# Two more token tiles through the VectorE transpose, one weight unit fewer prepared early, and a new instruction order

## The chip, the cores and the metric

One core of one Trainium2 chip. The metric is the time of one execution on the device in microseconds (us), lower is better. Three executions of the kernel before took 564.96, 565.62 and 566.87 us; the median is 565.62 us.

## The reference

The input x has 2048 tokens of 512 features. It is normalised over the features; the result goes through a linear attention block without a causal mask (32 heads of 16), and, beside it, through a gated feed-forward block of 1792 hidden features. The output is x plus the product of the two.

```
xn  = layernorm(x)                              # 2048 x 512
q, k, v = split(xn @ wqkv), 32 heads of 16
pq, pk = phi(q), phi(k)                         # phi(t) = (t + 1 if t > 0 else exp(t)) + 1e-6
kv  = sum over tokens of pk^T v, per head       # 16 x 16 each
z   = sum over tokens of pk
o   = (pq @ kv) / (pq . z + 1e-6)
s   = o @ wo
g   = silu((gelu(xn @ w_gate) * (xn @ w_up)) @ w_down)   # 512 -> 1792 -> 512
out = x + s * g
```

## The kernel before

**Numbers and products.** All large products are made from float32 values that are split into a high part (a ScalarE cast) and a low part (a VectorE or GpSimd subtraction); each product is three matmul passes: high by high, high by low, low by high. Most products are also done by a seven-product scheme for two-by-two blocks (Strassen in Winograd's form), so that many tiles are sums and differences of blocks, made on GpSimd, VectorE and ScalarE. `PRODUCTS` names the seven; their sums are built in the PSUM banks X, Y and Z, with ScalarE copies that carry one bank over to another (`seed`, `saved`, `esaved`).

**First stage (0 to about 130 us).** The 16 tiles of 128 tokens are taken as eight pairs n = 0 to 7; pair n holds the tiles of `tokens[n]`, so pair 3 is tiles 3 and 7. For each tile: `load_x` brings x in; `ln` makes the statistics on VectorE and the normalised tile `xn` (VectorE for pairs 0 and 1, ScalarE after that); `transp` turns xn, so that features lie on partitions (`xt`); `split_x` and `forms` make the high and low parts of xt and of its block sums T (into `Xh`, `Xl`); `rest`, `first_products` and `plain` make k and q; `gacc` adds up the product of pk with xn over all tokens (banks `gps`), from which kv and z follow. Two ways to turn a tile exist:

- n < TX: four TensorE transposes into a PSUM tile `pt` and a ScalarE copy of it to `xt`.
- n >= TX: xn is stored to DRAM (`xn_d`), loaded back with its rows in another place (`xq`), and `squares`, one VectorE instruction that transposes 32 x 32 blocks, gives `xt`.

Pairs listed in `XA` are turned by TensorE but normalised on ScalarE.

**Weights of the feed-forward.** The gate and up matrices are used in 14 units q = 0 to 13 of 256 columns (even: gate, odd: up). A unit is made by `sums_w` (one load, four GpSimd sums) and four splits (ScalarE high, VectorE low). The units in `EARLY` are made by `prep_early` during the first stage, through small tiles `we`, and stored to `w_d` in eight pieces; `prep_w` later loads each with one DMA. The other units are made by `prep_w` where they are first used, in one of three buffers, and then stored whole to `w_d`. All 14 are loaded from there in the second half.

**Feed-forward (from about 124 us on).** `ffn(1, ...)` treats 1024 tokens with units 0 to 13, `ffn(0, ...)` the others with units 14 to 27, which are the same weights loaded again. `quad` makes one unit's products (banks FX, FY, FZ), the gelu and the gate-by-up tiles h; `prep_d` and `down_strassen` make the down product of each pair of units (banks dX, dY, dZ, sums `acc`). Beside it, `den` and `turn` prepare the attention's denominator and the turned pq for each tile, and `attn` and `out_tile` finish the output.

**Order.** `Plan.do` records each operation with a number in the order in which the code makes it. The list `ORDER` at the head of the file then gives the sequence of these numbers; each engine's instructions, TensorE's among them, and all DMA issues (every one on SP's queue) are emitted in it. So an engine's queue is the list cut down to its own operations, and an instruction that waits holds back what is behind it on its engine. The `due` times in the code play no part once ORDER is fixed.

Of the kernel before, what the change touches and what calls it, by code (L numbers as in the profile page):

```python
# [292 lines left out]
def kernel(  # L293
# [242 lines left out]
    TX = 4  # L536
# [4 lines left out]
    def load_next():  # L541
        if xq:
            load_x(xq.pop(0))

    xns = {}
    XA = [(2, 6), (3, 7)]

    def ln(*ts):
        n = len(ts)
# [378 lines left out]
    EARLY = range(11,14)  # L928
# [539 lines left out]
```

## Time and profile before

| what | value |
|---|---|
| median of three runs | 565.62 us (564.96 to 566.87) |
| the profiled execution: time | 565.26 us |
| the profiled execution: span of its instructions | 563.3 us |
| granted TensorE clock, mean | 0.999 of full speed |
| VectorE, ScalarE, GpSimd busy | 86%, 63%, 39% of the span |
| DMA traffic | 143.71 MB, 255 GB/s over the span |

The profile calls TensorE PE (its weight loads PEld), VectorE DVE, ScalarE ACT and GpSimd POOL; SP issues the DMAs. `L442 PE ... FX<-Xh,w` is an instruction of line 442 that writes the tile FX and reads Xh and w; lines 398, 404 and 442 are helpers, so that tiles say more than lines. A row of a group gives the number of instructions, their durations in ns (least, median, most, or the mean), and times in us from the start of the span. Matmuls are pipelined: each is recorded with 379 ns, and they start some 215 ns apart.

### The profile page before, as it was taken

Reading aid. Unit: us, or ns where it says so; the run is one execution under the profiler, and the core shown is the slowest. Engines: PE = TensorE matmul, PEld = TensorE weight load, DVE = VectorE, ACT = ScalarE, POOL = GpSimd, SP = SyncE. Lnnn points to the kernel's source line nnn. Section 1 sums busy time; section 2 is a strip of 40 time slices with the busy share of each in tenths; the row PEclk is TensorE's granted clock in tenths of the full one; section 3 lists DMA queues with packets and bytes.
Section 4 is the critical chain, followed back from the end, with each engine's and each line's share of the span. In section 5 each row is a group of like instructions: output and inputs, shape, how many; then the busy total and the mean of one; then the engine's idle time right before and its main releaser. Section 6 shows DMA issues by size and latency. Waiting matters only on the chain.

```text
span 563.3 us, 7910 instructions
## 1 busy us (share of the span) xinstructions
PE 556.6 (99%) x2616; PEld 486.8 (86%) x2616; DVE 485.6 (86%) x769; ACT 356.3 (63%) x650; POOL 221.7 (39%) x245
## 2 busy tenths in 40 slices
PE   8999999999999999999999999999999999999997
PEld 7888888888988888888888888888888888888886
DVE  6999898876889889999998876985899696899997
ACT  5998868768477876654456275888536354565541
POOL 4636173346684675503563532130122221235200
PEclk9999999999999999999999999999999999999999
DMA  7449899889959872589575998798966726167767
GB/s 271 143 112 300 265 318 296 269 242 331 345 178 376 285 311 76 204 317 343 187 291 188 372 398 295 285 302 307 298 222 221 268 79 240 52 211 254 269 235 252
DMA packets 82362, 143.71 MB, mean 255 GB/s; under 512 B 5393, under 2 KB 50449, under 8 KB 78354
## 3 DMA queue, kind: packets, MB, share of 16 engines
q1 hardware_dynamic: 82322, 143.22, 73.9%
q8 instruction: 20, 0.33, 0.2%
q14 instruction: 20, 0.16, 0.1%
HBM read 89.19 MB, written 54.00 MB: 254 GB/s over the span
## 4 chain that ended last, share of the span: by engine, by line
PE 94%; DVE 4%; ACT 1%; issue 1%; DVEq 0%; ACTq 0%
PE FX L442 25%; PE dX L442 12%; PE FZ L442 12%; PE gps L442 7%; PE dY L442 6%; PE FY L442 6%; PE sps L442 6%; PE X L442 6%; PE dZ L442 3%; PE Z L442 3%; PE k L442 2%; PE q L442 2%; PE Y L442 1%; PE warm L472 1%; DVE acc L404 1%; DVE acc L1128 1%
## 5 line engine op out<-in xcount | busy, mean ns | idle before, releaser
L442 PE MATMUL FX<-Xh,w 128*128 128x512 f32 x448 | 126.4, 379 | 0.8 <-ACT fu L398 0.5
L442 PEld LDWEIGHTS FX<-Xh,w 128*128 128x128 f32 x448 | 84.5, 189 | 13.5 <-ACT fu L398 0.9
L1174 POOL TENSOR_TENSOR h<-h,g 128x512 f32<-128x512 f32 x28 | 39.2, 1401 | 135.4 <-DVE h L404 85.2
L398 ACT COPY dY<-dX 128x512 f32<-128x512 f32 x56 | 32.1, 573 | 61.7 <-DVE acc L1128 40.4
L442 PE MATMUL FX<-Xl,w 128*128 128x512 f32 x224 | 66.1, 379 | 0.0
L442 PE MATMUL FZ<-Xh,w 128*128 128x512 f32 x224 | 65.0, 380 | 0.0
L398 ACT COPY fu<-FX 128x512 f32<-128x512 f32 x56 | 32.7, 585 | 26.4 <-PE FX L442 19.7
L442 PEld LDWEIGHTS FZ<-Xh,w 128*128 128x128 f32 x224 | 42.2, 189 | 6.3 <-issue 0.4
L442 PEld LDWEIGHTS FX<-Xl,w 128*128 128x128 f32 x224 | 42.3, 189 | 6.0
L404 POOL TENSOR_TENSOR tmp<-raw 128x256 f32<-128x256 f32 x28 | 25.4, 914 | 52.5 <-DVE we L404 28.1
L404 POOL TENSOR_TENSOR sums<-draw 128x256 f32<-128x256 f32 x28 | 25.1, 900 | 50.1 <-DMA draw<-in_B_w_down 27.6
L404 DVE TENSOR_TENSOR hfl<-sums,hfh 128x512 fp32r<-128x512 f32 x56 | 40.1, 723 | 3.0 <-ACT hfh L398 3.0
L442 PE MATMUL dX<-hfl,dh 128*128 128x512 f32 x112 | 42.0, 379 | 0.0
L442 PE MATMUL dX<-hfh,dh 128*128 128x512 f32 x112 | 41.9, 380 | 0.0
L1128 DVE TENSOR_TENSOR acc<-acc,dX 128x512 f32<-128x512 f32 x48 | 32.5, 682 | 10.5 <-PE dX L442 10.3
L442 PE MATMUL dX<-hfh,dl 128*128 128x512 f32 x112 | 41.3, 379 | 0.0
L1128 DVE TENSOR_TENSOR acc<-acc,dY 128x512 f32<-128x512 f32 x48 | 32.6, 679 | 9.1 <-PE dY L442 9.1
L398 ACT CAST hfh<-sums 128x512 fp32r<-128x512 f32 x56 | 33.9, 617 | 7.1 <-DVE sums L404 5.7
L442 PE MATMUL FZ<-Xl,w 128*128 128x512 f32 x112 | 33.3, 379 | 0.0
L404 DVE TENSOR_TENSOR hfl<-h,hfh 128x512 fp32r<-128x512 f32 x42 | 30.0, 716 | 3.8 <-ACT hfh L398 2.5
L442 PE MATMUL FY<-Xh,w 128*128 128x512 f32 x112 | 32.7, 379 | 0.0
L398 ACT CAST hfh<-h 128x512 fp32r<-128x512 f32 x42 | 25.6, 618 | 7.3 <-PE dY L442 5.3
(221 smaller groups left out, 1475.7 us busy)
## 6 DMA issues: line engine op xcount, KB each, us to landing
w<-w_d SPq DMA_DIRECT2D x17, 1792.0 KB, 8.8
w_d<-w SPq DMA_DIRECT2D x11, 1792.0 KB, 9.2
draw<-in_B_w_down SPq DMA_DIRECT2D x14, 512.0 KB, 4.5
w_d<-we SPq DMA_DIRECT2D x18, 256.0 KB, 3.5
x<-in_A_x SPq DMA_DIRECT2D x16, 256.0 KB, 3.4
q_d<-qp SPq DMA_DIRECT2D x16, 256.0 KB, 3.9
qz<-q_d SPq DMA_DIRECT2D x16, 256.0 KB, 3.0
q<-q_d SPq DMA_DIRECT2D x16, 256.0 KB, 3.8
```

The source lines that it names most:

```text
L398: do("ACT", act(n, src.psum), lambda o, i: nc.scalar.copy(o, i), dst, src, name=name)
L404: do(eng, c, lambda o, p, q: getattr(e, f"tensor_{op}")(o, p, q), dst, a, b, name=name)
L442: nc.tensor.matmul(o if r is None else o[:, r], a, turned(b), start=first, stop=made == self.passes[r], skip_group_check=self.on or r is n ...
L472: nc.tensor.matmul(o, w, w, start=True, stop=True)
L1128: do("DVE", dve(D), lambda o, i: nc.vector.tensor_add(o, o, i), o, ps, name="acc")
L1174: do("POOL", pool(NC), lambda o, i: nc.gpsimd.tensor_mul(o, o, i), h, g, name="h")
```

## The change

Four things differ: `TX` is 3, so that pair 3 (tiles 3 and 7) is turned by way of DRAM and VectorE; `XA` loses that pair, since its normalisation now goes by the branch for n >= TX (also on ScalarE); `EARLY` is units 12 and 13, and unit 11 is made by `prep_w`, stored to `w_d`, in the feed-forward; and `ORDER` is another list, of 3615 entries in place of 3621. The entry numbers shift with the operations that come and go, and nearly every line of the list differs. Its first and last lines stand here for all:

```diff
 ORDER = [
-    3, 8, 0, 1, 4, 5, 6, 11, 10, 12, 56, 9, 7, 57, 58, 17, 15, 59, 16, 18, 60, 14, 19, 90, 20, 89, 22, 13, 92, 23, 94, 116, 21, 28, 100, 29, 118, 62,
...
+    3, 8, 0, 4, 959, 5, 6, 10, 11, 12, 56, 7, 9, 57, 1, 58, 17, 16, 59, 14, 18, 19, 60, 15, 20, 90, 89, 22, 21, 13, 94, 23, 28, 62, 61, 95, 63, 65,
...
+    3590, 3601, 3599, 3605, 3606, 3591, 3600, 3603, 3612, 3592, 3602, 3613, 3609, 3614, 3610, 3611,
 ]
...
     CL = 2
-    TX = 4
+    TX = 3
...
     xns = {}
-    XA = [(2, 6), (3, 7)]
+    XA = [(2, 6)]
...
-    EARLY = range(11,14)
+    EARLY = range(12,14)
     WHEN = (90, 140)
```

No function is new.

283 rows, old and new, of the table ORDER are left out of this document.

## The prediction

> **What bounds the kernel now.** I read the page first: span, busy times, the chain's shares. Then the waits of TensorE, the chain in order of time, and busy time by stretches.
>
> ```profile
> span 563.3 us, 7910 instructions
> PE 556.6 (99%) x2616; PEld 486.8 (86%) x2616; DVE 485.6 (86%) x769; ACT 356.3 (63%) x650; POOL 221.7 (39%) x245
> PE 94%; DVE 4%; ACT 1%; issue 1%; DVEq 0%; ACTq 0%
> ```
>
> TensorE is busy in 556.6 of 563.3 us, and 94% of the chain is its own. So a change is worth what it takes out of TensorE's instructions, plus what it alters in TensorE's few waits. Those are:
>
> ```profile
> PE warm L472 <- DVE neg_half L464: 1.1, 1, 1.1
> PE k L442 <- ACT b L398: 0.8, 1, 0.8
> PE FX L442 <- ACT fu L398: 0.5, 1, 0.5
> PE FX L442 <- ACT FY L398: 0.2, 1, 0.2
> ```
>
> The reader sees 1.5 us that a new order could win (0.8 in the front, 0.5 + 0.2 in the first feed-forward half); the 1.1 us ahead of the warm-up and the drain behind the last matmul stay. The chain, in order of time, shows where the 0.5 came from and what eight transposes cost:
>
> ```profile
> 12.39 0.87 PE pt L655 x8
> ...
> 285.42 1.69 DVE sums L404
> 287.14 0.62 ACT hfh L398
> 287.81 0.59 ACT fu L398
> 288.45 2.43 PE FX L442 x10
> ```
>
> A VectorE subtraction took 1.69 us, a ScalarE cast stood behind it, the copy that empties bank X behind that, and TensorE waited. VectorE is the second bound. In the rows below the columns are stretch, length, then busy time of PE, PEld, DVE, ACT, POOL:
>
> ```profile
> 15.00:30.00 15.00, 15.00 (x73) 13.13 (x73) 14.94 (x30) 14.56 (x28) 9.24 (x15) 1.00 0.50 144
> 30.00:45.00 15.00, 15.00 (x77) 13.17 (x76) 14.37 (x27) 14.22 (x24) 5.55 (x8) 1.00 0.43 115
> 180.00:200.00 20.00, 20.00 (x95) 17.50 (x94) 16.81 (x25) 16.80 (x34) 12.59 (x13) 1.00 0.79 274
> 200.00:220.00 20.00, 20.00 (x94) 17.53 (x93) 19.14 (x26) 13.97 (x28) 11.23 (x11) 1.00 0.66 253
> 220.00:240.00 20.00, 20.00 (x94) 17.50 (x93) 19.19 (x32) 12.27 (x23) 13.62 (x14) 1.00 0.40 145
> 240.00:260.00 20.00, 20.00 (x95) 17.50 (x94) 19.20 (x32) 10.90 (x20) 2.94 (x2) 1.00 0.92 330
> 260.00:280.00 20.00, 19.75 (x92) 16.80 (x91) 18.84 (x30) 8.99 (x17) 9.30 (x9) 1.00 0.70 232
> 280.00:300.00 20.00, 19.46 (x91) 16.73 (x90) 17.86 (x28) 10.80 (x21) 10.91 (x9) 1.00 0.79 293
> ```
>
> VectorE is nearly full in two places, 15 to 45 and 200 to 280, and the waits of 0.2 and 0.5 us lie at the end of the second.
>
> **How I read the new order.** Numbering the operations as the code makes them names every entry of both lists. Adding the trace's own durations along one engine's entries gives a count of work, no run: the *TensorE place* of an entry is the TensorE time listed ahead of it.
>
> **Part 1: pair 3 (tiles 3 and 7) by squares.**
>
> ```profile
> L655 PE MATMUL pt<-blk,xn x32: 272/273/273, 6.8 to 44.5; 128*128 128x128 f32 x32
> L398 ACT COPY xt<-pt x8: 573/590/621, 11.7 to 45.2; 128x512 f32<-128x512 f32 x8
> L629 DVE STREAM_TRANSPOSE xt<-xq x8: 1053/1095/1116, 49.6 to 102.7; 128x512 f32<-128x512 f32 x8
> ...
> x<-in_A_x SPq DMA_DIRECT2D x16, 256.0 KB, 3.4
> ...
> xn_d<-xn SPq DMA_DIRECT2D x8, 256.0 KB, 3.9
> xq<-xn_d SPq DMA_DIRECT2D x8, 256.0 KB, 3.2
> ```
>
> Four transposes per tile, 32 for eight tiles; two tiles fewer are eight, 0.87 us by the chain's row, all on TensorE's path: **-0.87**. ScalarE loses two copies (2 x 0.590 = 1.18), VectorE gains two squares (2 x 1.095 = 2.19), SP gains two stores and two loads. The new list puts the second store at TensorE place 32.7 and the squares at 41.4 and 42.7. Between lie 3.9 + 3.2 = 7.1 us of landing and two issues of some 0.4, so the round trip is covered by about 1 us; DMA share is 0.43 there. If that cover goes, the first square stands at VectorE's head with all of VectorE's queue behind it, and products of pair 2 wait: up to 1 us. On GpSimd the clearing of a column of tile 3's xn (place 35.9) now waits for that tile's store (31.8, landed some 4 us later); the next on GpSimd is pair 3's own T form, at 42.7. On SP the four issues stand among loads of x; the load that is held up longest, by the wait for the store, is at place 37.5, its tile's statistics at 49.4, and 3.4 us of landing fit. GpSimd's T forms follow the squares as they followed the copies. VectorE's 2.19 lies in its full stretch, which I price with the front.
>
> **Part 2: weights of unit 11 made in the feed-forward.**
>
> ```profile
> L404 POOL TENSOR_TENSOR tmp<-raw 128x256 f32<-128x256 f32 x28 | 25.4, 914 | 52.5 <-DVE we L404 28.1
> ...
> L404 DVE TENSOR_TENSOR w<-tmp,w x22: 677/688/1756, 123.6 to 249.7; 128x512 fp32r<-128x512 f32 x22
> L404 DVE TENSOR_TENSOR w<-raw,w x22: 412/679/1168, 117.9 to 246.5; 128x512 fp32r<-128x512 f32 x11, 128x256 fp32r<-128x256 f32 x11
> ...
> w<-w_d SPq DMA_DIRECT2D x17, 1792.0 KB, 8.8
> w_d<-w SPq DMA_DIRECT2D x11, 1792.0 KB, 9.2
> ```
>
> The same work moves from TensorE places 45 to 69 to places 230 to 280: four GpSimd sums (4 x 0.914 = 3.7), four ScalarE casts, four VectorE subtractions (2 x 0.688 + 0.679 + 0.412 = 2.47). SP loses eight small stores and one load of 1.8 MB and gains one store of it (9.2 us to land, at place 286; the next user of that buffer, unit 14's load, is at 310). What leaves the first stage wins nothing there, since TensorE does not wait between 10 and 265 us. What arrives could cost up to 2.47: in 200 to 260 the three rows leave VectorE 2.5 us free, in all three so thinly that little can be moved into them. But the new list takes other VectorE work out: two `den` reductions go from places 224 and 223 to 181 and 191, where the row leaves 3.2 free, and four `turn` pairs from 245 to 267 to 237 to 253. Counted along the lists, VectorE holds 58.7 of 60 us in 200 to 260 (58.1 before), 18.2 in 260 to 280 (18.7) and 19.9 in 280 to 300 (18.1). The tightest place: from the last matmul of a `dX` sum (first row half of the down product of units 2 and 3, place 221) to unit 9's first product (place 231), VectorE's queue holds 10.2 us, from the addition of that sum to the `h` whose release the product needs, where TensorE has 9.7. So a wait of about 0.5, one like it of 0.2 near 205, and some 0.3 of hand-over for each: 1.3 us. Against that, some durations counted there are stretched ones (rival C shows one); at the medians the queues would be shorter than TensorE's work and the wait nil. I take 1.2 us of waits where before had 0.7: **+0.5**. Ends: -0.7 (all gone) and +3.0 (rival C).
>
> **Part 3: the front, new order.** A slice, with idle time in brackets:
>
> ```profile
> 7.17 1.03 DVE L585 TENSOR_SCALAR xn<-x,mv,rstd 128x512 f32<-128x512 f32 x1
> 7.40 0.37 ACT L398 CAST Xh<-pt 128x256 fp32r<-128x256 f32 x1 [0.88 <-PE pt L655]
> 7.67 0.38 ACT L398 CAST b<-pt 128x256 fp32r<-128x256 f32 x1
> 8.19 0.45 PE L442 MATMUL k<-kq,b 128*128 128x512 f32 x1 [0.83 <-ACT b L398]
> 8.48 0.60 PE L655 MATMUL pt<-blk,xn 128*128 128x128 f32 x4
> 9.54 1.12 PE L442 MATMUL k<-kq,Xh 128*128 128x512 f32 x3
> ```
>
> TensorE waits 0.83 for the cast to b, behind another cast; the second tile's transposes come after. The new list puts b's cast first, that tile's normalisation ahead of another tile's statistics, and both tiles' transposes before any product, so the gap can fill with work. At most 0.83 is won. But counted to the first q products, VectorE's queue then leaves TensorE only 0.2 to 0.3 us (1.3 to 1.5 before), and it holds the 2.19 of squares soon after: I take half, **-0.4**; ends -0.83 and +0.5.
>
> **The rest.** From 310 us on no TensorE wait over 0.03 us shows, and the last two half sums are only swapped: 0, ends -0.1 and +0.5.
>
> **Sum.** -0.87 - 0.4 + 0.5 = -0.8: span 563.3 to 562.5. The profiled run took 565.26, 1.96 around its span; the median of the three is 565.62, 0.36 above it. From the median: **564.8 us**.
>
> **Rivals.** *B, all of it works:* -0.87 - 0.83 - 0.7 = -2.4, 563.2. For it: each of the waits has one named cause that the order can move. Against: the counts above.
> *C, slower: VectorE becomes TensorE's bound in 200 to 300.* For it:
>
> ```profile
> 285.17 1.38 POOL L965 TENSOR_TENSOR qz<-qz,zq 128x512 f32<-128x512 f32 x1
> 285.34 1.76 DVE L404 TENSOR_TENSOR sums<-h,sums 128x512 f32<-128x512 f32 x1
> ...
> L404 DVE TENSOR_TENSOR sums<-h,sums x28: 675/685/1760, 169.4 to 530.2; 128x512 f32<-128x512 f32 x28
> ```
>
> The subtraction that started inside GpSimd's multiplication took 1.76 instead of 0.685. Unit 11's four sums now run beside a full VectorE; if each stretches a VectorE instruction by its length, that is up to 3.7 us, less about 0.7 that the stretched ones there now give back: +3.0 for +0.5, so 567.3, and to 568.3 with the front's +0.5. It decides once waits there exceed about 3.7 us in all. Against: most instructions beside GpSimd keep 0.685, the median.
> [...]
> *D, the transposes' 0.87 buys nothing,* because VectorE, full at 15 to 45, sets the first stage and takes the 2.19 more: -0.4 + 0.5, so 565.7. [...] Against D: eight tiles go this way already, and no wait of TensorE follows them.
>
> **Chances.** "Same" is within 0.3%, 1.7 us, about what a measurement of this kernel can tell. The forecast, with D's 0.15, 0.49; B, or enough of it to pass -1.7, 0.28; C 0.23. So faster 0.28, same 0.49, slower 0.23. Range 563.0 to 567.9: from B nearly to C's end.
>
> **What would show it.** 24 transposes in PE's pt row and ten squares; PE busy near 555.7; TensorE's wait for b gone or halved; TensorE's waits in 200 to 330 listed behind DVE's `h`, `acc` or `sums`, 1 to 1.5 us in sum; den reductions before 195. Wrong if a DMA (xq, w or draw) appears among TensorE's releasers, if VectorE stretched by GpSimd costs over 3 us, or if waits appear after 330.

## The result, and the profile after

Six executions of the kernel after took 562.45 to 565.12 us, median 563.33; six of the kernel before 564.96 to 567.46, median 566.52. The ratio is 0.9949, 95% interval 0.9927 to 0.9971: faster by 2.9 us. That is beyond the 1.7 us that I had called "same". The time lies in the range, 0.3 us above its lower end: it is the time of rival B (563.2), not that of the forecast (564.8).

The profiled execution happens to be the slowest of the six, 565.12 us with a span of 563.1. Its page, first lines and chain shares:

```profile
span 563.1 us, 7880 instructions
...
PE 555.3 (99%) x2608; PEld 485.2 (86%) x2608; DVE 496.0 (88%) x771; ACT 354.2 (63%) x648; POOL 222.5 (40%) x245
...
PE 91%; DVE 4%; DMA 2%; issue 1%; SPq 0%; POOL 0%; DVEq 0%; POOLq 0%
```

TensorE has eight instructions less and is busy 1.3 us less (555.3; near 555.7 was expected). VectorE is busy 10.4 us longer (485.6 before), of which the two squares explain 2.2. TensorE's waits in this execution:

```profile
PE pt L655 <- DVE xn L585: 1.3, 1, 1.3
PE warm L472 <- DVE blk L462: 1.1, 1, 1.1
PE dX L442 <- DVE fifth L1128: 1.1, 1, 1.1
```

The waits for b, and for ScalarE's copies in 265 to 290, are gone. Two others have come, 1.3 us at 8 us and 1.1 us at 520 us, neither in a place that I had named. A second profile of the same kernel (the first experiment) has neither. Groups by tile and busy time by stretches (PE, PEld, DVE, ACT, POOL), kernel after:

```profile
L655 PE MATMUL pt<-blk,xn x24: 272/273/328, 6.2 to 27.9; 128*128 128x128 f32 x24
...
L629 DVE STREAM_TRANSPOSE xt<-xq x10: 1087/1098/1120, 42.3 to 98.1; 128x512 f32<-128x512 f32 x10
...
L404 DVE TENSOR_TENSOR sums<-h,sums x28: 662/684/1754, 167.8 to 527.9; 128x512 f32<-128x512 f32 x28
```

```profile
15.00:30.00 15.00, 15.00 (x75) 12.97 (x74) 14.64 (x30) 14.83 (x29) 9.91 (x17) 1.00 0.59 172
30.00:45.00 15.00, 15.00 (x70) 12.76 (x69) 14.97 (x26) 13.17 (x22) 6.10 (x9) 1.00 0.61 178
...
200.00:220.00 20.00, 20.00 (x94) 17.55 (x93) 18.54 (x28) 13.33 (x26) 13.58 (x14) 1.00 0.59 220
220.00:240.00 20.00, 20.00 (x94) 17.45 (x94) 19.55 (x33) 12.93 (x25) 12.28 (x14) 1.00 0.56 226
240.00:260.00 20.00, 20.00 (x95) 17.53 (x94) 19.84 (x31) 10.68 (x21) 6.71 (x6) 1.00 0.49 131
```

VectorE is nearly as full as counted, 57.9 of 60 us in 200 to 260 (58.7 was counted) and 19.84 of 20 in its last third, and yet TensorE has no idle time in any of these stretches: VectorE, busy for 97% of 200 to 260, cost TensorE no wait there. In the place that the prediction found tightest VectorE was even ahead: it waited 0.23 us for TensorE there (and 0.23 at 226.78 in after_again).

```profile
227.80 0.69 DVE L1128 TENSOR_TENSOR acc<-acc,dX 128x512 f32<-128x512 f32 x1 [0.23 <-PE dX L442]
```

To compare executions I use one count. Of TensorE's 2552 matmuls that are neither warm-up nor transposes I take the starts of number 20, 1000 and 1600, counted from 0 (they lie near 14, 222 and 352 us) and the end of the last, each less 0.109 us for every transpose ahead of it (0.87 us for the eight in the chain's row of before). The differences are TensorE's time for an equal number of matmuls, waits included, in us. Each row is one execution, the one that was profiled:

| execution | to the 20th | 20th to 1000th | 1000th to 1600th | to the end |
|---|---|---|---|---|
| before | 13.09 | 208.19 | 131.21 | 203.40 |
| after, profiled first | 12.62 | 209.12 | 129.81 | 204.74 |
| after_again | 12.27 | 208.45 | 130.20 | 203.14 |
| squares_back | 12.52 | 208.51 | 129.95 | 203.14 |
| old_front | 12.92 | 209.02 | 130.12 | 203.14 |
| front_on_dve | 12.03 | 208.48 | 129.72 | 203.14 |
| before_new_front | 11.92 | 208.80 | 130.35 | 203.13 |
| late_new | 13.05 | 211.01 | 129.70 | 203.14 |
| no_unit11 | 11.85 | 208.77 | 132.70 | 203.14 |
| no_unit11b | 12.51 | 208.52 | 130.84 | 203.13 |
| late_new_loaded | 13.12 | 208.74 | 135.84 | 203.13 |

### The profile page after: what moved, and what is told of

Read it like the earlier page. It is cut to its first block, busy times and chain, and to the rows that moved or that the text cites. A ratio compares the mean times of both kernels' runs of the same rounds, so it can differ in the third digit from the quotient of the medians.

```text
span 563.1 us, 7880 instructions
## 1 busy us (share of the span) xinstructions
PE 555.3 (99%) x2608; PEld 485.2 (86%) x2608; DVE 496.0 (88%) x771; ACT 354.2 (63%) x648; POOL 222.5 (40%) x245
## 4 chain that ended last, share of the span: by engine, by line
PE 91%; DVE 4%; DMA 2%; issue 1%; SPq 0%; POOL 0%; DVEq 0%; POOLq 0%
PE FX L442 26%; PE FZ L442 13%; PE dX L442 12%; PE gps L442 7%; PE FY L442 6%; PE dY L442 6%; PE X L442 6%; PE sps L442 3%; PE dZ L442 3%; PE Z L442 3%; PE k L442 2%; PE q L442 2%; PE Y L442 1%; DMA out_yT<-g 1%; DVE acc L1128 1%
## 5 line engine op out<-in xcount | busy, mean ns | idle before, releaser
L404 POOL TENSOR_TENSOR sums<-draw 128x256 f32<-128x256 f32 x28 | 23.2, 837 | 69.1 <-DMA draw<-in_B_w_down 46.1
L404 DVE TENSOR_TENSOR hfl<-sums,hfh 128x512 fp32r<-128x512 f32 x56 | 46.6, 837 | 0.7 <-ACT hfh L398 0.5
L404 DVE TENSOR_TENSOR hfl<-h,hfh 128x512 fp32r<-128x512 f32 x42 | 32.0, 763 | 0.2
```

What stands on the lines that cost most here:

```text
L404: do(eng, c, lambda o, p, q: getattr(e, f"tensor_{op}")(o, p, q), dst, a, b, name=name)
```

## Experiments

Three theories are tested. Theory 1 is the prediction's sum with its better ends: the transposes, the front and the waits in 200 to 300 us each give back what they cost. Theory 2 says that the waits at 8 and 520 us are meetings of VectorE and GpSimd that other executions don't have. Theory 3 says that the new order stands only with the move of unit 11. D is the prediction's rival. "Place" is TensorE time listed ahead of an entry, as there. Each ratio is to the kernel before on the same chip, with its 95% interval. The runs were made on three chips, on which the kernel before had medians of 565.40, 565.39 and 565.54 us, so medians are compared across them too.

**after_again.** The kernel after once more, without an edit.

> The kernel after, unchanged, for a second profile beside the three below. Theory 1 (the sum of the prediction with better ends: transposes -0.87, the waits of 0.24 + 0.54 us in 265 to 290 gone, and the rest a matter of the front): ratio 0.995 to the kernel before, the wait of about 1.3 us in the front there again. Theory 2 (the waits of 1.3 us in the front and 1.1 us at 520 us in the profiled execution are chance meetings of VectorE and GpSimd, which other executions don't have): same ratio, but at least one of the two waits is gone or under half, and the span is 560.4 to 562 us.

562.77 us, 0.9953 (0.9940 to 0.9965). Span 560.5. Besides the wait of 1.1 us ahead of the warm-up, TensorE has one wait:

```profile
PE dX L442 <- DVE hfl L404: 0.3, 1, 0.3
```

The front, first in the kernel after's first profile, then here (timeline: start, length; the GpSimd row of the first joins two instructions):

```profile
5.37 0.62 ACT L398 CAST kq<-wk 128x512 fp32r<-128x512 f32 x1 [3.31 <-DMA wk<-in_A_wqkv]
...
6.58 2.67 POOL L404 TENSOR_TENSOR kq<-wk,kq 128x512 fp32r<-128x512 f32 x2
...
6.64 1.48 DVE L585 TENSOR_SCALAR xn<-x,mv,rstd 128x512 f32<-128x512 f32 x1 [0.46 <-POOL rstd L558]
...
8.18 0.66 PE L655 MATMUL pt<-blk,xn 128*128 128x128 f32 x4 [1.28 <-DVE xn L585]
```

```profile
6.28 0.62 ACT L398 CAST kq<-wk 128x512 fp32r<-128x512 f32 x1 [4.22 <-DMA wk<-in_A_wqkv]
...
6.51 0.55 DVE L585 TENSOR_SCALAR xn<-x,mv,rstd 128x512 f32<-128x512 f32 x1 [0.46 <-POOL rstd L558]
...
6.98 1.27 POOL L404 TENSOR_TENSOR kq<-wk,kq 128x512 fp32r<-128x512 f32 x1 [0.50 <-DMA wk<-in_A_wqkv]
```

In the slower one the weights landed 0.9 us earlier. So GpSimd's subtraction started 0.06 us ahead of the second xn instead of 0.47 behind it; xn took 1.48 us, and the second transposes waited 1.28. In the eight profiles that have this front, xn took 1.48 in five, where the subtraction came first (ScalarE's cast at 5.03 to 5.37 us), and 0.55 in three (cast at 5.91 to 6.28). The first k product began at 8.81 to 9.04 or at 7.86 to 8.37. The wait at 520 us is in one profile of all: `sums` and `g` there took 1.75 and 1.76 us beside GpSimd's `dl`. Theory 2 holds for both: the first comes and goes with the landing of the weights, the second came once.

**squares_back.** Pair 3 by TensorE again, its entries at the old places:

```diff
-    TX = 3
+    TX = 4
...
-    XA = [(2, 6)]
+    XA = [(2, 6), (3, 7)]
```

> The kernel after with pair 3 turned by TensorE again (32 transposes, eight squares), its instructions at the places that the kernel before gave them; all else stays. Theory 1 (the transposes bound TensorE): 0.87 us slower than the kernel after, 564.2 where that has 563.3. Rival D (VectorE sets 15 to 45 us, so it gains what two squares of 1.1 us cost): within 0.3 us of the kernel after, and less idle time of TensorE between 10 and 60 us.

563.76 us, 0.9974 (0.9964 to 0.9984): 1.0 us over after_again by the medians, 1.2 +- 0.9 by the ratios. Its profile has the front's meeting too:

```profile
PE warm L472 <- DVE blk L462: 1.1, 1, 1.1
PE pt L655 <- DVE xn L585: 0.9, 1, 0.9
```

In the table its 20th to 1000th matmul takes 208.51, against 208.45 in after_again: in this pair of executions the two squares cost TensorE nothing, and the transposes' 0.87 is won in full. Rival D, for which squares_back was to lie within 0.3 us of the kernel after, falls, though by the ratios only just.

**weights_back and order_alone.** Unit 11 goes into the first stage again, under TensorE's new order, with the instructions of units 11 to 13 placed anew; order_alone also has squares_back's edit.

```diff
-    EARLY = range(12,14)
+    EARLY = range(11,14)
```

> The kernel after with unit 11's weights made in the first stage again and loaded in the feed-forward; TensorE's order stays, and the instructions of units 11 to 13 are put into the first stage where the queues have most room. Theory 1 (the move gives and costs nothing by itself): within 0.3 us of the kernel after. Theory 3 (the new order of the first stage has no room for a third unit, so the move is what lets it stand): TensorE waits in 40 to 140 us, 1 to 3 us in all, so 564.5 to 566.

> The new order alone: TensorE's order of the kernel after, with 32 transposes and eight squares, and with unit 11's weights made in the first stage as before. Theory 1: 0.87 us over the kernel after, 564.2, so two thirds of the gain. Theory 3 (the order needs the move): 565.5 to 567, with TensorE waiting in 40 to 140 us. If the order gives nothing and the two other parts carry the gain: 566.5, the time before, with the waits of 0.24 and 0.54 us in 265 to 290 us there again.

588.29 us, 1.0402 (1.0381 to 1.0423), and 597.33 us, 1.0570 (1.0544 to 1.0596): far beyond every theory. ScalarE's waits in 38 to 135 us, and busy time by stretches around one wait of TensorE, of weights_back:

```profile
ACT we L399 <- DMA w_d<-we: 15.4, 5, 4.8
```

```profile
83.00:86.20 3.20, 0.19 (x2) 0.10 (x1) 2.01 (x5) 1.30 (x3) 0.00 (x0) 1.00 0.14 52
86.20:88.00 1.80, 1.80 (x6) 1.04 (x7) 1.80 (x5) 1.80 (x4) 1.58 (x3) 0.77 0.88 282
88.00:90.00 2.00, 2.00 (x6) 1.53 (x6) 2.00 (x4) 1.96 (x5) 2.00 (x4) 0.50 0.83 270
```

ScalarE stood 15.4 us before casts into `we`, each behind the store that empties the tile, with all its other work queued behind. TensorE waited 3.0 us, and then ran at half its clock (0.50 in the row of 88 to 90). These two show that three units, as I packed them, don't fit into the new first stage; they don't price the order. How the 23 and 32 us come together wasn't followed further.

**order_alone2.** This is order_alone with the entries of units 11 to 13 spread wider.

> The new order alone once more: 32 transposes, unit 11's weights in the first stage as before, TensorE's order of the kernel after; this time the instructions of units 11 to 13 are spread with a landing of 4 us allowed for every store, since in the two kernels before ScalarE's casts waited up to 4.8 us for the store that empties their buffer. Theory 1 (order and transposes carry the gain, the move none): 563.7, 0.9 over the kernel after. Theory 3 (the new order has no room for a third unit in the first stage): waits of TensorE in 40 to 160 us of 1 us and more, 565 or above.

592.28 us, 1.0461 (1.0440 to 1.0481). ScalarE again waited 15.1 us for those stores. Whether some other placement of a third unit fits the new order stays open.

**old_front.** ORDER only: the old list up to place 12 us, then the new one.

```diff
 ORDER = [
-    3, 8, 0, 4, 959, 5, 6, 10, 11, ...    (new order, to place 12 us)
+    (the same operations in the old order)
     ... the new order
```

> The kernel after with the front of the kernel before: every instruction up to TensorE place 12 us in the old order, all behind it in the new one. Theory 1 (the new front wins 0.4 to 0.8 us): 0.4 to 0.8 us slower than the kernel after, so 563.2 to 563.6 where that has 562.8, with the wait for b of about 0.8 us there again. Rival (what the new front wins is given back whenever GpSimd stretches the second xn): within 0.2 us of the kernel after.

563.89 us, 0.9978 (0.9967 to 0.9989): 1.1 us over after_again by the medians (1.4 +- 0.9 by the ratios). TensorE's wait in the front is 1.1 us here, and not for b, as was expected:

```profile
PE k L442 <- POOL kq L404: 1.1, 1, 1.1
```

The table has 0.65 us of the difference before the 20th matmul and 0.57 behind it. The second figure is no more than the kernel after's two executions differ by there (209.12 and 208.45), so it need not be the front's.

**front_on_dve.** One subtraction of the front moved from GpSimd to VectorE, where it stands behind the second xn:

```diff
-        kq_split(0, wk1, k, eng="DVE" if k else "POOL")
+        kq_split(0, wk1, k)
```

> The kernel after with one subtraction of the front (the low part of kq, first half) on VectorE, behind both xn, not on GpSimd. Theory 2 (GpSimd's subtraction, when its operand lands early, starts before the second xn and stretches it from 0.55 to 1.48 us, and TensorE's second transposes wait 0.9 to 1.3 us): no such wait in the profile, under 0.3 us in all before 10 us; the time 0.2 to 0.5 us below the kernel after if the meeting comes in about half the executions, the same if it is rare. Rival (VectorE's 0.68 us more delays b by as much): a wait behind b, 0.3 us or more slower.

562.03 us, 0.9940 (0.9928 to 0.9952), span 559.8. The only wait of TensorE that the profile lists, then rows of the front:

```profile
PE warm L472 <- DVE blk L462: 1.1, 1, 1.1
```

```profile
6.61 0.55 DVE L585 TENSOR_SCALAR xn<-x,mv,rstd 128x512 f32<-128x512 f32 x1 [0.46 <-POOL rstd L558]
7.07 0.69 DVE L404 TENSOR_TENSOR kq<-wk,kq 128x512 fp32r<-128x512 f32 x1
```

The subtraction takes 0.69 us here, where GpSimd took 1.27, and fills a hole in which VectorE waited for ScalarE. The weights landed late in this execution (ScalarE's cast at 6.39 us), so the meeting would not have come anyway; that it can't come follows from the subtraction's place behind xn. This version beats the kernel before, and it has the lowest median of all; against the kernel after, 0.7 us by the medians, the intervals still overlap. Whether it beats that too stays open.

**no_unit11.** Unit 11 isn't made, and unit 12's stored weights are loaded in its place, so this kernel leaves out a part of the work:

```diff
-        if q in EARLY:
+        if q in EARLY or q == 11:
...
-            dma(w.map(lambda ap: ap.bitcast(F32)), w_d(q), 2220)
+            dma(w.map(lambda ap: ap.bitcast(F32)), w_d(max(q, 12)), 2220)
```

> The kernel after without the making of unit 11's weights: unit 12's stored weights are loaded in their place in both row halves, so unit 11's share of the output is another; four GpSimd sums, four ScalarE casts, four VectorE subtractions and one store are left out. Theory 1 (what arrives in the feed-forward is hidden behind TensorE): within 0.2 us of the kernel after. The prediction's price for it (+0.5, VectorE nearly full in 200 to 280): 0.3 to 0.5 us faster than the kernel after, with the wait of about 0.3 us near 273 gone.

567.22 us, 1.0020 (1.0004 to 1.0036): with less work, 4.4 us slower than after_again. VectorE's and TensorE's waits, then SP's issues, of no_unit11:

```profile
DVE q L1235 <- DMA q<-q_d: 2.6, 1, 2.6
...
PE dX L442 <- DVE acc L1128: 2.1, 1, 2.1
```

```profile
240.35 0.44 SPq L394 DMA_DIRECT2D w<-w_d  x1
240.84 0.44 SPq L394 DMA_DIRECT2D q<-q_d  x1
```

The q of 256 KB was issued 0.5 us behind a load of 1.8 MB. VectorE could use it at 249.59 us, 8.7 us later; in after_again, without that load, a q issued at 240.66 was there before 247.32, when VectorE came to it. VectorE stood, and with it the addition to `acc` that empties bank dX. The profiled execution is the fastest of twelve (564.64 us); what the others, up to 568.26, lost on top isn't seen. Seven of them, 566.96 to 568.26, have a mean granted clock of 0.997, the five faster ones 0.998 to 1.000; one fall of the clock, as the last section shows it, would make such a difference by my estimate (3.41 us at 0.50 are 0.003 of the span), so it is a likely part of the loss, though none of these seven was profiled.

**no_unit11b.** This is no_unit11 with the load one DMA issue later, behind that q.

> no_unit11 once more (unit 12's stored weights loaded in place of unit 11's, which are not made), with one change: the 1.8 MB load stands behind the small load of q, not ahead of it. If the place of the load made no_unit11 4 us slower than the kernel after (VectorE waited 2.6 us for a q issued 0.5 us behind the load, TensorE 2.1 us behind VectorE): 562.5 to 563, at most 0.3 us from the kernel after, and no wait of TensorE over 0.5 us near 250. If it is anything else that the load brings: 565 or above again.

563.62 us, 0.9969 (0.9956 to 0.9982): 3.6 us less than no_unit11, from the place of one DMA issue alone. TensorE's wait there is now

```profile
PE FZ L442 <- DVE h L404: 0.5, 1, 0.5
```

since the next store behind the load, `t_d` from `sums`, still held VectorE 1.3 us. So making unit 11 in the feed-forward costs nothing that shows: without it, and with the load at this better place, the kernel is no faster than after_again (0.9 +- 1.0 us slower).

**late_new.** The old list up to place 140 us, then the new one, with TX = 4 and EARLY = range(12,14).

> The old order up to TensorE place 140 us (old front, 32 transposes, eight squares), the new one behind it, with unit 11's weights made in the feed-forward. Theory 1 (the late part's new order and the move win the losses of about 1.0 us in 250 to 350 and 0.3 near 386): 1.0 to 1.3 us faster than the kernel before, 564.1 to 564.4 where that has 565.4. If the late part gives nothing and front and transposes carry it all: 565.4, with waits in 265 to 290 again.

565.84 us, 1.0003 (0.9991 to 1.0015): no gain. The table splits it: the 1000th to 1600th matmul take 129.70, 1.5 us less than before, as theory 1 has it; but the 20th to 1000th take 211.01, 2.8 more. Of these, 1.6 lie in the old part (a wait of 0.55 at 54 us among them) and 1.2 in 140 to 222, behind the seam of the two lists. The profiled execution is the slowest of the twelve, and late_new_loaded, with the same seam, takes 208.74 there: how much of the 2.8 is the seam's and how much chance isn't shown. So the late part wins locally; what the late order wins by itself in a whole kernel isn't measured.

**late_new_loaded.** This is late_new with EARLY = range(11,14). In the kernel that ran, the load came to stand ahead of the small transfers, not behind as the expectation says.

> The same, but without the move: unit 11's weights made in the first stage as before and loaded in the feed-forward, the load of 1.8 MB put behind the small load of q that stands next to it. If the order alone wins the late part: 564.1 to 564.4, the same as with the move. If the new order needs the move (VectorE, then TensorE, waiting for a q or for the weights): 565 or above, with a wait of TensorE of 0.5 us or more in 240 to 290.

570.14 us, 1.0073 (1.0045 to 1.0100). VectorE's and TensorE's waits, and SP's issues:

```profile
DVE sums L630 <- DMA t_d<-sums: 3.4, 1, 3.4
...
PE FX L443 <- ACT FY L399: 2.7, 1, 2.7
```

```profile
240.87 0.32 SPq L395 DMA_DIRECT2D w<-w_d  x1
241.93 0.37 SPq L395 DMA_DIRECT2D t_d<-sums  x1
```

The store issued 1.1 us behind the load held VectorE's next squares 3.4 us, and TensorE 2.7. It is no_unit11's mechanism on another tile, 4.3 us slower than late_new: the new late order, with `turn` and `den` earlier, doesn't bear the load at this place, and the move is what takes it away. In the old order the same load, issued at 240.07, had 8.5 us before the next q (248.61).

**before_new_front.** The kernel before with the new front and front_on_dve's edit.

> The kernel before with the front of the kernel after, up to TensorE place 12 us, and the one subtraction of it on VectorE (as front_on_dve); all behind it in the old order. Theory 1 (the front is worth what its waits were, 0.8 to 1.1 us, wherever it stands): 564.3 to 564.6 where the kernel before has 565.4, no wait over 0.3 us before 10 us, the waits of 0.2 and 0.5 us in 265 to 290 there still. Rival (VectorE's queue behind the front is full, so the gain is given back by 45 us): 565.2 or above.

564.96 us, 0.9989 (0.9975 to 1.0004), between the two expectations, with a scatter of 563.35 to 567.21; 0.6 us below the kernel before by the medians, not clear of nothing. The front itself gains 1.2 us in the table (11.92 for 13.09), and half is lost again by the 1000th matmul. The profiled execution is the fastest of the twelve. In this execution of the old late order, TensorE's wait in 200 to 320 us was

```profile
PE FX L443 <- ACT FY L399: 0.2, 1, 0.2
```

where the kernel before's profile had 0.2 and 0.5. So part of the mid waits were chance as well.

## Why the prediction was right, and where not

The table adds up. From the kernel before's profile to after_again's, TensorE's time changes by -0.82 us to the 20th matmul, +0.26 to the 1000th, -1.01 to the 1600th and -0.26 to the end; with -0.87 for the transposes that is -2.7, and the spans differ by 2.8. So the forecast's -0.8 held inside its range, near the lower end, with one of its three terms right; what came is nearly rival B's sum of -2.4, to which I gave 0.28.

**The transposes, -0.87: right.** squares_back gives 1.0 to 1.2 +- 0.9, the 24 transposes and ten squares are in the trace, and VectorE's fuller 15 to 45 us (14.64 and 14.97 of 15) cost TensorE nothing. No DMA stands among TensorE's releasers; the round trip's cover of 1 us held.

**The front, -0.4: too small.** old_front says about -1.1 +- 0.9, which still includes -0.4. The table is sharper: to the 20th matmul the five executions with the front as the kernel after has it (after, after_again, squares_back and the two no_unit11) take 12.35 us in the mean, the four with the old front 13.05, so -0.7, most of the 0.83 that could be won. The step that failed is "VectorE's queue then leaves TensorE only 0.2 to 0.3 us ... I take half": the new front won more than half in spite of that queue. And the risk was looked for in the wrong place: I counted VectorE's queue with xn at its usual length, though the quoted rows of the front have an xn of 1.03 us and rival C's rows show a like case. The loss in five of eight executions, about 0.9 us at the first k product and 0.5 by the 20th matmul, came from a meeting with GpSimd, as in rival C, but at 6.6 us and not in 200 to 300.

**VectorE's waits in 200 to 300, +0.5: wrong sign.** The profile after has no wait of TensorE there, after_again one of 0.3. The table's 1000th to 1600th take 129.70 to 130.20 in the six executions of the new late order with unit 11 made there, 131.21 and 130.35 in the two of the old: -0.9 in the mean. The two old ones differ by as much, so the size is uncertain, but both lie above all six. The step that failed is the queue of "10.2 us ... where TensorE has 9.7": in both profiles of the kernel after VectorE waits 0.23 us for TensorE in that stretch, so its queue was the shorter one. The likely reason is that the durations came from one execution with its stretched instructions, which I said could make the wait nil; the length of that queue in other executions wasn't measured. By medians, 2.63 us of gain (565.40 - 562.77) less 0.99 and 1.12 leaves 0.5 for this part and the rest, with +- 0.9 on each of the two. How much of it is the new order's and how much the missing load's stays open.

**What the move is for: missed.** I named that SP loses "one load of 1.8 MB" and gave it no price. no_unit11 and late_new_loaded show that this load costs 4.4 and 4.3 us by the medians where it stands just ahead of small transfers of the new order; one DMA issue later, in no_unit11b, it costs 3.6 less. The work that took its place is hidden: no_unit11b, which leaves it out, is no faster.

**Rival C: its mechanism yes, its place no.** VectorE's busy time grew by 10.4 us in the profiled execution and by 5.0 in after_again (490.6), for some 2 us more work. Of the kernel after's two profiled executions only the slower one made TensorE pay for it by more than 0.3 us, at 8 and at 520 us. **The rest, 0:** right but for the 1.1 us at 520 in that one execution; the 0.26 us behind the 1600th matmul look like chance too, since before_new_front, with the old list there, has 203.13 like the others.

How long xn took in the front went with which started first, xn or GpSimd's subtraction: 1.48 us with the subtraction 0.06 us ahead, 0.55 with it 0.47 us behind. Why, no run here shows.

## What to carry to other kernels

Price a removed DMA by what stands behind it in the one queue: a 1.8 MB transfer 0.5 us ahead of a small one that an engine waits for cost 4.4 us more here than making its data anew on engines that had room (no_unit11). Where a short critical instruction takes longer beside another engine's, as xn did here (1.48 us for 0.55), ask whether the other engine can start first, and take the choice away (another engine, a place behind it) rather than hope for the better order. And one profile is one draw: the waits of 1.3 us at 8 us and 1.1 us at 520 us in the profile after were absent in after_again's, so a sum of such waits needs two profiles.

## What the runs showed of the hardware

TensorE's clock fell behind some of its waits. Behind nine waits of 2.55 to 3.58 us, in four of these kernels (weights_back, order_alone, order_alone2, late_new_loaded), seven or eight matmuls started some 0.43 us apart, not 0.216 (granted clock 0.50 in weights_back's row of 88 to 90 us), which cost 1.5 to 1.7 us more; behind three of 2.06, 2.28 and 2.41 us, and all shorter ones, the clock stayed full. A count in steps of the clock tells them apart as well. Up to the last matmul, the granted clock in every trace here changes only at whole steps of 3.41 us from the moment at which it is first full, and each slow stretch is one step long. Counted in these steps, all nine in which TensorE was idle for 2.04 us or more are followed by a step at 0.50, and none of those with 1.89 us or less. The wait of 2.41 us lay across the border of two steps, with some 1.2 us in each. Two pairs of such steps of order_alone (the last figure but two is the clock):

```profile
78.83:82.24 3.41, 1.52 (x7) 1.37 (x8) 2.68 (x7) 0.79 (x2) 0.22 (x1) 1.00 1.06 308
82.24:85.66 3.42, 3.42 (x18) 2.90 (x16) 1.59 (x3) 0.39 (x1) 0.41 (x1) 1.00 0.48 158
...
157.34:160.75 3.41, 1.37 (x6) 1.24 (x7) 0.00 (x0) 1.98 (x3) 0.00 (x0) 1.00 0.04 11
160.75:164.17 3.42, 3.42 (x9) 2.70 (x9) 0.39 (x1) 2.06 (x5) 0.00 (x0) 0.50 0.57 141
```

In late_new_loaded the late store made TensorE wait 2.7 us and lose 1.6 more behind that wait (granted clock 0.50 from 253 to 255 us), 4.3 in all.
